# First loads in one queue in order of need, first gate matmuls by halves of K, parameters transposed once

## The chip, the cores and the metric

The kernel runs on one core of a Trainium2 chip. The metric is the device time in microseconds of that core. The TensorE clock granted by the throttle was 1.0. This record does not show PE's slow start: it reads 1.00 between 3 and 4 us in the kernel before, where matmuls of 512 columns still start 0.43 us apart. So PE's clock is read here from the spacing of its matmuls. A profile gives the same execution in detail: PE is the matmul engine, DVE the vector engine, ACT the scalar engine (ScalarE), POOL the Pool engine and SP the engine that issues most DMAs (SyncE). Profile times start about 1.8 us after the measured time does, so 180.6 us measured is a span of 178.8 us.

## The reference

One layer with two branches on the same normalized input, 2048 tokens of 512 channels:

```python
xn = _layernorm(x, axis=-1)
return x + _A_ref(xn, ...) + _B_ref(xn, w_gate, w_up, w_down)
# _B_ref: (silu(xn @ w_gate) * (xn @ w_up)) @ w_down, inner width 1376
# _A_ref: a diagonal complex state-space layer: two input projections, a scan over the
#         2048 steps, two output projections, a skip term
```

## The kernel before

The tokens are handled in four chunks of 512. A small static scheduler in the kernel file builds a graph of tasks. PE and SP run their tasks in the order in which they are added; the orders on ACT, DVE and POOL are chosen by the scheduler from estimated durations, then fixed. Each engine takes its list in that order, so a task that waits holds everything behind it.

The head, the part in question, works on chunk 0. Each x tile has 128 tokens. DVE computes its statistics, POOL the inverse standard deviation, DVE the normalized tile; PE transposes it into PSUM; ACT evacuates that to `xnT`. In four "quarters" (one per x tile) PE then multiplies six tiles of `wg` (`w_gate`) with the tile.

Some words used below: K is the dimension that a matmul sums over, here 512 channels in four pieces of 128. An evacuation copies a result of PE out of its PSUM bank, so that the kernel can use the bank again. Warm-up (or bridge) matmuls multiply constants and their results are thrown away; they fill PE's time while it waits for the first loads. "Landed" is when all of a load had arrived.

```python
dma("ld_x0", ...)                                   # SP queue: x0 x1 x2 wg0 x3 wu0 ...
dma("ld_x1", ...)
act_load("ld_wgA0", wg[:, 0:2, 0:FQ], ...)          # ACT queue, 256 KB: first half of K, 4 tiles
dma("ld_x2", ...)
act_load("ld_wgA1", wg[:, 2:4, 0:FQ], ...)          # ACT queue, 256 KB: second half of K
dma("ld_wg0", wg[:, :, FQ:FH0], ...)                # tiles 4 and 5
dma("ld_x3", ...)
# two of three small parameter loads follow on the ACT queue
...
# ffn_gate_quarters, shortened
for q in range(4):
    for ii, (i, bk) in enumerate(tiles):            # six tiles
        if q == 0 and ii == 2:
            params_t(tiles[-1][1])                  # three parameter transposes
        if q < 3 and ii == (4 if q == 0 else 2):
            xt_tile_fine(q + 1)                     # transposes of the next x tile
        # four matmuls of 128x128x128; they need both wg halves
```

Two parts far behind the head:

```python
# a DMA transpose waits for all DMAs before it; a DMA after it waits for the transpose
if xpose:
    after = after + tuple(dma_tasks)
elif xp_state[0] is not None:
    after = after + (xp_state[0],)
...
loads_stage_b1()        # two DMA transposes (B_re, B_im)
xt_chunk_dma(1)         # one DMA transpose (x of chunk 1)
loads_stage_b2()        # two DMA transposes (C_re, C_im), then ld_x8: x of chunk 2
...
def ln_apply_act(a0):   # chunks 2 and 3: normalization on ACT
    # DVE: nmr = -mean * rstd
    for a in range(a0, a0 + 4):
        # ACT: xn_sb[a] = x_sb[a] * rstd + nmr
```

Of the kernel before, what the change touches and what calls it, by code (L numbers as in the profile page):

```python
# [19 lines left out]
    warm=10,  # L20
# [218 lines left out]
def bass_parallel_sum__ssm_conv_s5__swiglu_ffn__prompt_kernel(  # L239
# [32 lines left out]
    with es:  # L272
# [46 lines left out]
        prow = sb("prow", [4, 3, 128], B16)  # L319
# [76 lines left out]
        def pload(name, slot, src, order=()):  # L396
            return dma(name, prow[:, slot, :], src.rearrange("(a p) -> a p", p=128), [("prow", slot)], 1024, eng="act", order=order)
        FQ = 4 * 128
        act_q = [pload("ld_ldt", 2, A_log_dt)]

        def act_load(*args):
            act_q.append(dma(*args, eng="act", order=(act_q[-1],)))
# [3 lines left out]
        act_load("ld_wgA0", wg[:, 0:2, 0:FQ], wg_v[:, 0:2, 0:FQ], [("wg", "a0")], 256 * FQ * 2)  # L406
        dma("ld_x2", x_sb[:, 2:3, :], x_v[:, 2:3, :], [("x", 2)], TILEB)
        act_load("ld_wgA1", wg[:, 2:4, 0:FQ], wg_v[:, 2:4, 0:FQ], [("wg", "a1")], 256 * FQ * 2)
        dma("ld_wg0", wg[:, :, FQ:FH0], wg_v[:, :, FQ:FH0], [("wg", 0)], 512 * (FH0 - FQ) * 2)
        dma("ld_x3", x_sb[:, 3:4, :], x_v[:, 3:4, :], [("x", 3)], TILEB)  # L410
        act_q.append(pload("ld_lim", 1, A_Lambda_im, (act_q[-1],)))
        act_q.append(pload("ld_lre", 0, A_Lambda_re, (act_q[-1],)))
# [41 lines left out]
        def params_t(slot):  # L454
            def tr(e):
                for k in range(3):
                    inst = e.transpose(out=ptr[:, slot, 4 * k:4 * k + 4], in_=prow[0:4, k, :], identity=ident[0:4, 0:4])  # L457
                return inst
            g.add("pe", tr, reads=[("prow", k) for k in range(3)] + [("ident",)], writes=BK(slot), name="parT", est=100, ninst=3)

        def params_ev(slot, order):
            return g.add("dve", lambda e: e.tensor_copy(out=praw[:].rearrange("p k a -> p (k a)"), in_=ptr[:, slot, 0:12]),
                         reads=BK(slot), writes=[("praw", k) for k in range(3)], name="parTev", est=80, order=order)
# [17 lines left out]
        def ln_apply(a, parts=1, order=()):  # L481
            w = D // parts
            for h in range(parts):
                cs = slice(h * w, (h + 1) * w)
                last = g.add("dve", lambda e, a=a, cs=cs: e.tensor_scalar(out=xn_sb[:, a % NXN, cs], in0=x_sb[:, a, cs], scalar1=mv[:, a, 0:1], scalar2=rstd[:, a:a + 1],
                                                                          op0=ALU.subtract, op1=ALU.mult),
                             reads=[("x", a), ("mv", a), ("rstd", a)], writes=([("xn", a % NXN)] if h == parts - 1 else []) + ([("xh", h)] if parts > 1 else []),
                             name="xn%d" % a, est=90 + 260 // parts, order=order)
            return last
# [10 lines left out]
        def ln_chunk0():  # L500
            bn_st(0)
            bn_ag(0)
            last = ln_ve(0, 1)
            ln_rstd(0, 1)
            last = ln_apply(0, parts=2, order=(bn_st(1, order=(last,)),))
            last = ln_ve(1, 1, order=(bn_ag(1, order=(last,)),))
            ln_rstd(1, 1)
            return bn_st(2, order=(last,))

        def ln_chunk0_rest(last, par_bank):  # L510
            last = ln_apply(1, order=(last,))
            for a in range(2, 4):
                last = ln_ve(a, 1, order=(bn_ag(a, order=(last,)),))
                hold[a] = ln_rstd(a, 1)
                if a == 2:
                    last = params_ev(par_bank, (last,))
                last = ln_apply(a, order=(bn_st(a + 1, order=(last,)),) if a < 3 else (last,))
# [15 lines left out]
        def xt_tile_fine(a, parts=1, wbank=None):  # L533
            n = KT // parts
            for h in range(parts):
                if h:
                    pe_warm(1, 256, wbank)
                slot = xt_pair[0] + (a + h) % 2

                def tr4(e, h=h, slot=slot):  # L540
                    for j in range(n):
                        kt = h * n + j
                        inst = e.transpose(out=ptr[:, slot, j * 128:(j + 1) * 128],  # L543
                                           in_=xn_sb[:, a % NXN, kt * 128:(kt + 1) * 128], identity=ident[:])
                    return inst
                g.add("pe", tr4, reads=([("xn", a % NXN)] if h == parts - 1 else []) + ([("xh", h)] if parts > 1 else []) + [("ident",)], writes=BK(slot), name="xT%d" % a, est=n * 64, ninst=n)

                def evac(e, h=h, slot=slot):
                    return e.activation(out=xnT[:, 0, a % 4, h * n:(h + 1) * n, :],  # L549
                                        in_=ptr[:, slot, 0:n * 128].rearrange("p (k t) -> p k t", k=n), func=AF.Identity)  # L550
                g.add("act", evac, reads=BK(slot), writes=([("xnT", 0, a % 4)] if h == parts - 1 else []) + ([("xnT0", h)] if parts > 1 else []), name="xTev%d" % a, est=190 + 310 // parts)
# [68 lines left out]
        def params_b():  # L620
            dve_ts("thT", "thn", float(TP), ALU.mult)
            dve_range("thn")
            dve_range("thT")
            for i, n in enumerate(["lre", "lim"]):
                o = S(n)
                small("dve", n, lambda e, o=o, i=i: e.tensor_copy(out=o, in_=praw[:, i, :]), [("praw", i)], R(n))
            dve_tt("lam_re", "r", "cos_thn", ALU.mult)
            dve_tt("lam_im", "r", "sin_thn", ALU.mult)
            dve_ts("lm1", "lam_re", -1.0, ALU.add)
            dve_tt("lre2", "lre", "lre", ALU.mult)  # L630
            dve_tt("lim2", "lim", "lim", ALU.mult)
            dve_tt("den", "lre2", "lim2", ALU.add)
            o, a_ = S("rden"), S("den")
            small("dve", "rden", lambda e, o=o, a_=a_: e.reciprocal(out=o, in_=a_), R("den"), R("rden"))
            dve_tt("n1", "lm1", "lre", ALU.mult)
            dve_tt("n2", "lam_im", "lim", ALU.mult)
            dve_tt("n3", "n1", "n2", ALU.add)
            dve_tt("g_re", "n3", "rden", ALU.mult)
            dve_tt("n4", "lam_im", "lre", ALU.mult)
            dve_tt("n5", "lm1", "lim", ALU.mult)  # L640
            dve_tt("n6", "n4", "n5", ALU.subtract)
            dve_tt("g_im", "n6", "rden", ALU.mult)
            dve_ts("s_2gre", "g_re", 2.0, ALU.mult)
            dve_ts("s_m2gim", "g_im", -2.0, ALU.mult)
            dve_ts("s_m2gre", "g_re", -2.0, ALU.mult)
# [51 lines left out]
        def wres(nm, i):  # L697
            if nm == "wg" and i < 4:
                return [("wg", "a0"), ("wg", "a1")]
            return [(nm, 0 if i < 6 else 1)]  # L700
# [34 lines left out]
        def ffn_gate_quarters(pairs, last):  # L735
# [3 lines left out]
            xt_tile_fine(0, parts=2, wbank=banks[pairs[-1]])  # L739
            pe_warm(3, 256, banks[pairs[-1]])  # L740
            tiles = [(2 * ip + k, banks[ip] + k) for ip in pairs for k in range(2)]
            for q in range(4):
                for ii, (i, bk) in enumerate(tiles):
                    if q == 0 and ii == 2:
                        params_t(tiles[-1][1])
                        ln_chunk0_rest(last, tiles[-1][1])
                    if q < 3 and ii == (4 if q == 0 else 2):
                        xt_tile_fine(q + 1)
                    for k0, k1 in (((0, 2), (2, 4)) if q == 0 and ii == 0 else ((0, 4),)):
                        def mm(e, bk=bk, i=i, q=q, k0=k0, k1=k1):  # L750
                            for kt in range(k0, k1):
                                inst = e.matmul(pbank[:, bk, q * 128:(q + 1) * 128], lhsT=wg[:, kt, i * 128:(i + 1) * 128], rhs=xnT[:, 0, q, kt, :],  # L752
                                                start=(kt == 0), stop=(kt == KT - 1))
                            return inst
                        xr = [("xnT", 0, q)] if q else [("xnT0", h) for h in range((k1 + 1) // 2)]
                        g.add("pe", mm, reads=wres("wg", i) + xr, writes=BK(bk), name="mm_gq%d_%d" % (i, q), est=(k1 - k0) * 56, ninst=k1 - k0)
# [165 lines left out]
        if _CFG["warm"]:  # L922
            pe_warm(_CFG["warm"])
        ffn_gate_quarters([0, 1, 2], ln_chunk0())
# [106 lines left out]
```

## Time and profile before

Before the prediction: 180.56 us, median of 3 runs (180.40 to 181.02).

| what | value | where it is read |
|---|---|---|
| span of the profiled run | 178.8 us | first line of the page |
| PE busy | 174.5 us, 98% | engine shares |
| first gate matmul | 6.35 us | chain of waits |
| first up matmul | 13.05 us | timeline of PE |
| wait for an evacuation before quarter 1 | 0.41 us | spacing of PE's matmuls |

Two lines of the page of the kernel before: its span, and busy time with the share of the span for each engine.

```profile
span 178.8 us, 2346 instructions
PE 174.5 (98%) x908; PEld 82.9 (46%) x908; DVE 160.6 (90%) x272; ACT 86.5 (48%) x107; POOL 13.0 (7%) x24
```

The chain of waits of the kernel before, followed back from its end. Columns: start in us, length in us, what the end was waiting for.

```profile
1.80 4.42 DMA wg<-in_B_w_gate_dram
...
6.35 0.61 PE pb L752 x8
6.96 0.16 PE pb L457 x3
...
7.92 0.61 ACT xnT L549
...
8.58 0.62 PE pb L752 x8
...
10.98 2.23 PE pb L752 x40
13.22 12.09 PE pb L713 x56
...
41.83 8.74 PE pb L713 x40
50.57 0.04 issue
50.60 8.81 PE pb L713 x40
```

L752 is the gate matmuls of the quarters, L457 the parameter transposes, L549 the evacuation of a transposed x tile, L713 the later gate and up matmuls. The second wg half arrives at 6.2 us and the gates start; after a wait for ACT at 7.92 us everything seems to be PE.

### The profile page before, as it was taken

The page shows a single profiled execution, that of the slowest core. Times are in us where ns is not written, and L with a number is a line of the kernel's source. Part 1 is how long each engine was busy: PE and PEld are TensorE (multiplying, and loading weights), DVE is VectorE, ACT ScalarE, POOL GpSimd, SP SyncE. Part 2 cuts the span into 40 slices and gives each one's busy share as a digit, 9 for nine tenths or more (in the row PEclk, how much of TensorE's full clock was granted, in tenths as well). Part 3 has the DMA queues.
Part 4 walks back from the last instruction along what each step waited for, and adds up shares of the span by engine and source line. Part 5 has one row for each costly group of instructions (what it writes and reads, how often), then busy time and mean ns, then how long its engine had stood idle before and what let it go on. Part 6 is the DMA issues. An engine that isn't in the chain of part 4 may idle for free.

```text
span 178.8 us, 2346 instructions
## 1 busy us (share of the span) xinstructions
PE 174.5 (98%) x908; PEld 82.9 (46%) x908; DVE 160.6 (90%) x272; ACT 86.5 (48%) x107; POOL 13.0 (7%) x24
## 2 busy tenths in 40 slices
PE   8799999999999999999999999999999999999994
PEld 2594444444444444444444444444444444444643
DVE  3888759998799999999999999999999999999733
ACT  3379899899696992060565651000965620000000
POOL 3362300001300000210000000000000000000000
DMA  5995646669360000002330000001100000001212
GB/s 159 353 355 110 129 81 72 148 170 354 113 117 4 0 0 0 0 0 92 85 64 0 0 0 4 0 0 59 59 0 4 0 0 0 0 0 33 69 48 88
DMA packets 23410, 12.37 MB, mean 69 GB/s; under 512 B 15112, under 2 KB 23400, under 8 KB 23400
## 3 DMA queue, kind: packets, MB, share of 16 engines
q1 hardware_dynamic: 22832, 11.70, 24.6%
q10 hardware_dynamic: 568, 0.53, 1.0%
q8 instruction: 7, 0.11, 0.3%
q14 instruction: 3, 0.02, 0.0%
HBM read 6.46 MB, written 2.10 MB: 48 GB/s over the span
## 4 chain that ended last, share of the span: by engine, by line
PE 95%; DMA 2%; ACTq 1%; ACT 0%; DVE 0%; issue 0%
PE pb L713 36%; PE pb L900 21%; PE pb L913 15%; PE pb L818 15%; PE pb L752 3%; DMA wg<-in_B_w_gate_dram 2%; PE pb L781 2%; PE pb L791 1%; ACTq L385 1%; PE pb L543 0%; ACT xnT L549 0%; DVE x_sb L918 0%; PE pb L457 0%
## 5 line engine op out<-in xcount | busy, mean ns | idle before, releaser
L858 DVE TENSOR_TENSOR_SCAN rot<-sm,car,rot 128x512 bf16<-128x512 f32 x32 | 39.1, 1268 | 0.1
L900 PE MATMUL pb<-wd,hT 128*128 128x512 bf16 (+3 forms) x187 | 38.7, 367 | 0.0
L713 PE MATMUL pb<-xnT,wu 128*128 128x512 bf16 x160 | 37.3, 379 | 0.0
L713 PE MATMUL pb<-xnT,wg 128*128 128x512 bf16 x136 | 32.0, 380 | 0.0
L913 PE MATMUL pb<-W,hss 128*128 128x512 bf16 (+1 forms) x136 | 28.3, 367 | 0.0
L818 PE MATMUL pb<-xnT,BT 128*128 128x512 bf16 x128 | 28.1, 379 | 0.0
L900 PEld LDWEIGHTS pb<-wd,hT 128*128 128x128 bf16 (+1 forms) x187 | 18.2, 97 | 20.1
L725 ACT ACTIVATE sg<-pb 128x1024 bf16<-128x1024 f32 x20 | 20.2, 1021 | 10.5 <-PE pb L713 10.2
L713 PEld LDWEIGHTS pb<-xnT,wu 128*128 128x128 bf16 x160 | 15.5, 98 | 18.9 <-ACT uf L771 0.5
L771 ACT ACTIVATE uf<-pb 128x1024 bf16<-128x1024 f32 x20 | 20.4, 1021 | 7.1 <-PE pb L713 5.7
L713 PEld LDWEIGHTS pb<-xnT,wg 128*128 128x128 bf16 x136 | 13.1, 98 | 16.4 <-issue 0.8
L913 PEld LDWEIGHTS pb<-W,hss 128*128 128x128 bf16 x136 | 13.3, 98 | 14.4
L818 PEld LDWEIGHTS pb<-xnT,BT 128*128 128x128 bf16 x128 | 12.5, 98 | 15.1
L825 ACT ACTIVATE u_sb<-pb 128x1024 bf16<-128x1024 f32 x16 | 16.3, 1025 | 3.9 <-PE pb L818 3.5
L918 DVE TENSOR_TENSOR x_sb<-pb,x_sb 128x512 bf16<-128x512 f32 (+1 forms) x17 | 10.9, 655 | 5.0 <-PE pb L913 5.0
L773 DVE TENSOR_TENSOR hT<-sg,uf 128x1024 bf16<-128x1024 bf16 x20 | 13.4, 677 | 2.1 <-ACT uf L771 2.1
L466 DVE BATCH_NORM_STATS2 st<-x_sb 128x6 f32<-128x512 bf16 x16 | 10.2, 681 | 5.0 <-DMA x_sb<-in_A_x_dram 5.0
L495 ACT ACTIVATE xn_sb<-x_sb,nmr,rstd 128x512 bf16<-128x512 bf16 x8 | 5.9, 802 | 10.5 <-DVE nmr L492 10.5
L800 ACT ACTIVATE sg<-pb 96x1024 bf16<-96x1024 f32 x2 | 2.0, 1019 | 17.4 <-PE pb L781 17.4
L849 DVE TENSOR_TENSOR rot<-rot,sin 128x2048 bf16<-128x2048 bf16 x8 | 9.8, 1219 | 0.0
L849 DVE TENSOR_TENSOR rot<-u_sb,sin 128x2048 bf16<-128x2048 bf16 x8 | 9.7, 1218 | 0.0
L849 DVE TENSOR_TENSOR rot<-u_sb,cosT 128x2048 bf16<-128x2048 bf16 x8 | 9.7, 1215 | 0.0
(71 smaller groups left out, 138.8 us busy)
## 6 DMA issues: line engine op xcount, KB each, us to landing
out_dram<-x_sb SPq DMA_DIRECT2D x15, 128.0 KB, 1.7
x_sb<-in_A_x_dram SPq DMA_DIRECT2D x3, 512.0 KB, 7.5
wd<-in_B_w_down_dram SPq DMA_DIRECT2D x1, 1280.0 KB, 7.0
wu<-in_B_w_up_dram SPq DMA_DIRECT2D x1, 768.0 KB, 6.1
wg<-in_B_w_gate_dram SPq DMA_DIRECT2D x1, 608.0 KB, 7.5
wu<-in_B_w_up_dram SPq DMA_DIRECT2D x1, 608.0 KB, 8.6
x_sb<-in_A_x_dram SPq DMA_DIRECT2D x4, 128.0 KB, 2.8
wg<-in_B_w_gate_dram ACTq DMA_DIRECT2D x2, 256.0 KB, 3.8
```

Of the source, the lines that this page charges most:

```text
L466: return g.add("dve", lambda e, a=a: e.bn_stats(out=st[:, a, :], in_=x_sb[:, a, :]), reads=[("x", a)], writes=[("st", a)], name="bnst%d" % ...
L713: inst = e.matmul(pbank[0:fs, bk, :].rearrange("p (j t) -> p j t", j=4), lhsT=w[:, kt, i * 128:i * 128 + fs], rhs=xnT[:, c % 2, :, kt, :], ...
L725: g.add("act", lambda e: e.activation(out=sg[rows, sl, 0:n, :].rearrange("p a t -> p (a t)"), in_=pair_f32(rows, bk, 512 * n), func=AF.Sil ...
L771: g.add("act", lambda e: e.activation(out=uf[rows, ul, 0:n, :].rearrange("p a t -> p (a t)"), in_=pair_f32(rows, bk, 512 * n), func=AF.Ide ...
L773: g.add("dve", lambda e: e.tensor_tensor(out=hT[rows, hb, i0:i0 + n, :], in0=sg[rows, sl, 0:n, :], in1=uf[rows, ul, 0:n, :], op=ALU.mult), ...
L818: inst = e.matmul(pbank[:, bk, :].rearrange("p (j t) -> p j t", j=4), lhsT=BT[:, ri, kt, pt * 128:(pt + 1) * 128], rhs=xnT[:, c % 2, :, kt ...
L825: g.add("act", lambda e: e.activation(out=u_sb[:, us].rearrange("p r t -> p (r t)"), in_=pair_f32(slice(0, 128), b0), func=AF.Identity), r ...
L849: tt = lambda out, a, b, op, r, w, nm: g.add("dve", lambda e: e.tensor_tensor(out=out, in0=a, in1=b, op=op), reads=r, writes=w, name="%s_% ...
L858: g.add("dve", lambda e, A0=A0, A1=A1, k=k, ri=ri, pt=pt: e.tensor_tensor_scan(out=A1[:, k, ri, :], data0=rr[:, pt:pt + 1].to_broadcast([1 ...
L900: inst = e.matmul(pbank[:, bk, 0:nc_], lhsT=hT[0:fs, hb, i, lt * 128:(lt + 1) * 128], rhs=wd[0:fs, i, c0:c0 + nc_], start=(i == 0), stop=F ...
L913: inst = e.matmul(pbank[:, bk, 0:nc_], lhsT=hss[:, hb, pt, ri, lt * 128:(lt + 1) * 128], rhs=W12[:, ri, pt, c0:c0 + nc_], start=False, sto ...
L918: g.add("dve", lambda e, bk=bk, a=a, c0=c0, nc_=nc_: e.tensor_tensor(out=x_sb[:, a, c0:c0 + nc_], in0=pbank[:, bk, 0:nc_], in1=x_sb[:, a, ...
```

## The change

Its intent: issue the first loads in one queue in the order in which they are needed, so that no later load competes with an earlier one; let the first gate matmuls start when half of the first x tile and half of wg are there; and take the parameter transposes out of the gate matmuls. The diff, cut to its core:

```diff
-            return dma(name, prow[:, slot, :], ..., eng="act", order=order)
+            return dma(name, prow[4 * slot:4 * slot + 4, :], ..., eng="act", order=order)
         act_q = [pload("ld_ldt", 2, A_log_dt)]
+        act_q.append(pload("ld_lim", 1, A_Lambda_im, (act_q[-1],)))
+        act_q.append(pload("ld_lre", 0, A_Lambda_re, (act_q[-1],)))
         dma("ld_x0", ...)
         dma("ld_x1", ...)
-        act_load("ld_wgA0", wg[:, 0:2, 0:FQ], ...)
+        dma("ld_wgA0", wg[:, 0:2, 0:FH0], ...)       # 384 KB, all six tiles
         dma("ld_x2", ...)
-        act_load("ld_wgA1", wg[:, 2:4, 0:FQ], ...)
-        dma("ld_wg0", wg[:, :, FQ:FH0], ...)
+        dma("ld_wgA1", wg[:, 2:4, 0:FH0], ...)
         dma("ld_x3", ...)
...
+            pe_warm(8, bk=wbank)
+            params_t(pbk)                # one transpose of 12 rows instead of three of 4
+            ln_chunk0(pbk)               # DVE: xn0 half, bn_aggr and eps of tile 1, xn0 half
+            pe_warm(2, bk=wbank)
+            xt_tile_fine(0, bridge=wbank)
+            pe_warm(2, 256, wbank)
             for q in range(4):
-                for ii, (i, bk) in enumerate(tiles):
-                    if q == 0 and ii == 2:
-                        params_t(tiles[-1][1])
-                    if q < 3 and ii == (4 if q == 0 else 2):
+                if q < 3:
+                    steps = [(i, bk, 2 * kh, 2 * kh + 2) for kh in range(2) for i, bk in tiles]
+                else:
+                    steps = [(i, bk, 0, 4) for i, bk in tiles]
+                for n, (i, bk, k0, k1) in enumerate(steps):
+                    if q < 3 and n == 9:
                         xt_tile_fine(q + 1)     # now two halves: 2 transposes and an evacuation each
```

## The prediction

> **What bounds the kernel now.** Engine shares on the page: PE busy 174.5 of 178.8 us (98%). The chain of waits is PE alone from 10.98 to 176.33 us; PE's timeline has no gap after the first up matmul (13.05 us). DVE is 90% busy, but its last hss tile is ready near 164.8 us and first read at 169.2 us. So the change can win only in the first 13 us, and the win should reach the end.
>
> **The head before** (timeline and chain). Warm-up to 4.7 us; the first x tile transposed at 5.15 and 5.41 us; its second ScalarE evacuation ends at 6.13 us; the first gate matmul starts at 6.35 us, because the second half of wg landed at 6.2 us. Then 108 matmuls and transposes at 56 ns (6.04 us), parameter transposes (0.15 us), one wait for an evacuation (8.17 to 8.58 us, 0.41 us): 13.05 us.
>
> **What changes.**
> - Loads in one queue. The Trainium skill, "DMA: Bandwidth & Descriptors", section "Issuing engines are not separate DMA queues", says that queues share the same 16 engines; this trace agrees (320 to 390 GB/s with one queue or two). By bytes I estimate the wg halves at 4.5 to 4.8 and 5.7 to 6.2 us, needed at 6.0 and 6.7 us. The DMA wait goes, worth only about 0.2 us. The small loads (two landed at 6.6 and 6.8 us behind wg) land near 3 us, so they don't hold PE.
> - Parameter transpose moved into idle time: 0.15 us less on PE later.
> - DVE does bn_aggr and the eps add of tile 1 (0.18 and 0.15 us) between the halves of tile 0: the second half comes near 5.63 instead of 5.35 us. With two bridge matmuls behind it I estimate the first gate matmul at 6.02 us: 0.33 us earlier.
> - Transposes by halves. Before, 16 or more matmuls covered an evacuation (0.60 us) in later quarters. Now only 6 matmuls (0.34 us) follow the next tile's transposes. A half's evacuation takes 0.38 us and starts 0.3 us after its transposes: I estimate waits of 0.19 us before quarters 1 and 2. Quarter 3 runs with full K and needs both halves at once: about 0.48 us. Sum 0.86 against 0.41 us: 0.45 us given back.
>
> **Sum.** -0.33 - 0.15 + 0.45 = about 0; first up matmul at 12.9 us (12.6 to 13.4). Matmuls, DVE work and bytes stay the same; the static scheduler may reorder DVE and ACT, which DVE's slack should hide.
>
> **Predicted time** 180.3 us, range 179.7 to 180.9; chances: faster by over 2% 0.01, within 2% 0.96, slower 0.03.
>
> **What would show each step.** PE's timeline: first gate matmul near 6.0 us without a DMA wait; idle gaps before quarters 1, 2 and 3, the last the longest, put down to ScalarE; first up matmul 12.6 to 13.2 us; no gap afterwards. DVE: the first tile's second half at 5.3 us. DMA: the second wg half before 6.5 us.
>
> **What would make it wrong.** A single queue that starts slower (second wg half after 6.7 us). PE left at its slow clock: warm-up matmuls were 0.43 us apart until 4.1 us, 0.22 us after (the skill, "TensorE: Matmul & The Clock Gate", "What's actually happening", tells of half rate until some 3.4 us of activity; this trace agrees). ScalarE doing a table step (0.72 us) before the last x evacuation: quarter 3 would slip 0.7 us. A DVE order that uses up the hss slack.

## The result and the profile after

The changed kernel took 181.37 us, median of 6 runs (180.83 to 181.85); the kernel before 180.70 us (180.40 to 181.07, 6 runs). The ratio is 1.0033, with a 95% interval of 1.0015 to 1.0051. Ratios here are the mean time of one kernel's fast runs over that of the other's in the same rounds, so they are not quite the ratio of the medians. By the 2% rule that is "the same", as forecast; but the median lies 0.47 us above the range of the prediction. Two later measurements of the unaltered changed kernel gave 0.9993 (0.997 to 1.0015) and 1.0037 (0.9998 to 1.0077). Over all 18 runs of the changed kernel the mean is 181.20 us, over the 28 of the kernel before that stood beside them 180.84 us: the change costs about 0.2%.

The same two lines of the page, of the changed kernel:

```profile
span 179.1 us, 2337 instructions
PE 174.8 (98%) x897; PEld 83.2 (46%) x905; DVE 160.2 (89%) x271; ACT 86.8 (48%) x111; POOL 12.7 (7%) x24
```

(Eight matmul records are missing from this trace, which has 897 matmuls for 905 weight loads. The change itself takes away three, two parameter transposes and a warm-up.) The shares say nothing. The timeline of PE in the head of the changed kernel does; columns: start, length, engine, line, what, count, and in brackets idle time and what ended it. L536 is the transposes of x, L444 the warm-up matmuls, L752 the gate matmuls of the quarters, L707 the first up matmuls.

```profile
5.28 0.42 PE L536 MATMUL pb<-ident,xn_sb 128*128 128x128 bf16 x2
5.49 0.42 PE L444 MATMUL pb<-const-bfloat16-1.0 128*128 128x256 bf16 x1
5.70 0.42 PE L536 MATMUL pb<-ident,xn_sb 128*128 128x128 bf16 x2
5.92 0.62 PE L444 MATMUL pb<-const-bfloat16-1.0 128*128 128x256 bf16 x2
6.34 1.29 PE L752 MATMUL pb<-xnT,wg 128*128 128x128 bf16 x18
...
11.01 0.39 PE L536 MATMUL pb<-ident,xn_sb 128*128 128x128 bf16 x4
11.23 0.50 PE L752 MATMUL pb<-xnT,wg 128*128 128x128 bf16 x6
12.23 1.51 PE L752 MATMUL pb<-xnT,wg 128*128 128x128 bf16 x24 [0.50 <-ACT xnT L542]
13.58 0.59 PE L707 MATMUL pb<-xnT,wu 128*128 128x512 bf16 x2
```

Three things can be read. The gates start at 6.34 us, no earlier than before: PE is still at its slow clock (two warm-up matmuls of 256 columns take 0.43 us from start to start of the next, 0.21 each; at the full clock it was 0.11 each), so the two that stand ahead of the gates take twice as long. Behind the transposes at 11.01 us stand only six matmuls, then PE idles for ACT. And the first up matmul starts at 13.58 us, 0.53 us later than before.

The chain of waits of the changed kernel:

```profile
3.22 4.54 DMA x_sb<-in_A_x_dram
...
7.78 0.69 DVE st L457
...
9.15 0.55 POOL rstd L469
9.70 1.00 POOL sm L602
...
10.91 0.72 ACT scrC L654
11.63 0.55 ACT xnT L542 x2
...
12.23 1.51 PE pb L752 x24
13.74 12.09 PE pb L707 x56
...
42.35 17.37 PE pb L707 x80
```

The chain no longer begins with wg but with x3, the fourth x tile, issued at 3.22 us and landed at 7.76 us. Its statistics on DVE, two steps on POOL and the first step of a sine table on ACT (L654) follow; that table step stands ahead of the last x evacuation in ACT's list and delays it. In the last line the row of L707 from 42.35 us runs through 80 matmuls: the break near 50 us is not there.

What the 16 DMA engines moved, in stretches of 1 us. Columns: stretch, its length, busy time of each engine (instructions), PE clock, mean busy share of the DMA engines, GB/s. First the kernel before:

```profile
3.00:4.00 1.00, 1.00 (x4) 0.36 (x3) 0.93 (x4) 0.89 (x1) 0.00 (x0) 1.00 1.02 335
6.00:7.00 1.00, 0.68 (x12) 0.58 (x11) 0.89 (x4) 0.13 (x1) 0.27 (x1) 1.00 1.07 348
```

Then the changed kernel:

```profile
3.00:4.00 1.00, 1.00 (x4) 0.21 (x2) 0.93 (x4) 0.49 (x2) 0.00 (x0) 1.00 0.83 171
6.00:7.00 1.00, 1.00 (x16) 0.83 (x13) 0.87 (x2) 0.50 (x2) 0.05 (x1) 1.00 1.03 289
```

In this pair of profiles the loads start slower with one queue: 171 instead of 335 GB/s between 3 and 4 us. The second profile of the kernel before had only 247 GB/s there.

### The profile page after: what moved, and what is told of

It is laid out like the page before. It is cut to its first block, busy times and chain, and to the rows that moved or that the text cites. A ratio compares the mean times of both kernels' runs of the same rounds, so it can differ in the third digit from the quotient of the medians.

```text
span 179.1 us, 2337 instructions
## 1 busy us (share of the span) xinstructions
PE 174.8 (98%) x897; PEld 83.2 (46%) x905; DVE 160.2 (89%) x271; ACT 86.8 (48%) x111; POOL 12.7 (7%) x24
## 4 chain that ended last, share of the span: by engine, by line
PE 92%; DMA 3%; SPq 1%; DVE 1%; POOL 1%; ACT 1%; issue 1%
PE pb L707 36%; PE pb L901 21%; PE pb L819 15%; PE pb L914 15%; DMA x_sb<-in_A_x_dram 3%; PE pb L782 2%; SPq L384 1%; PE pb L792 1%; PE pb L752 1%; POOL sm L602 1%; ACT scrC L654 0%; DVE st L457 0%; ACT xnT L542 0%; POOL rstd L469 0%; DVE x_sb L919 0%
## 5 line engine op out<-in xcount | busy, mean ns | idle before, releaser
L901 PE MATMUL pb<-wd,hT 128*128 128x512 bf16 (+3 forms) x183 | 38.0, 366 | 0.2
L707 PE MATMUL pb<-xnT,wu 128*128 128x512 bf16 x160 | 37.3, 379 | 0.0
L707 PE MATMUL pb<-xnT,wg 128*128 128x512 bf16 x136 | 32.0, 379 | 0.0
L707 PEld LDWEIGHTS pb<-xnT,wu 128*128 128x128 bf16 x160 | 15.6, 98 | 18.7 <-ACT uf L772 0.2
L707 PEld LDWEIGHTS pb<-xnT,wg 128*128 128x128 bf16 x136 | 13.1, 98 | 16.4 <-issue 0.8
L914 PEld LDWEIGHTS pb<-W,hss 128*128 128x128 bf16 x136 | 13.3, 98 | 14.4
L774 DVE TENSOR_TENSOR hT<-sg,uf 128x1024 bf16<-128x1024 bf16 x20 | 13.3, 677 | 2.5 <-ACT uf L772 2.4
L481 ACT ACTIVATE xn_sb<-x_sb,nmr,rstd 128x512 bf16<-128x512 bf16 x8 | 5.9, 802 | 9.4 <-DVE nmr L478 9.4
L850 DVE TENSOR_TENSOR rot<-rot,cosT 128x2048 bf16<-128x2048 bf16 x8 | 9.7, 1214 | 0.0
```

Of the source, the lines that this page charges most:

```text
L707: inst = e.matmul(pbank[0:fs, bk, :].rearrange("p (j t) -> p j t", j=4), lhsT=w[:, kt, i * 128:i * 128 + fs], rhs=xnT[:, c % 2, :, kt, :], ...
L774: g.add("dve", lambda e: e.tensor_tensor(out=hT[rows, hb, i0:i0 + n, :], in0=sg[rows, sl, 0:n, :], in1=uf[rows, ul, 0:n, :], op=ALU.mult), ...
L850: tt = lambda out, a, b, op, r, w, nm: g.add("dve", lambda e: e.tensor_tensor(out=out, in0=a, in1=b, op=op), reads=r, writes=w, name="%s_% ...
L901: inst = e.matmul(pbank[:, bk, 0:nc_], lhsT=hT[0:fs, hb, i, lt * 128:(lt + 1) * 128], rhs=wd[0:fs, i, c0:c0 + nc_], start=(i == 0), stop=F ...
L914: inst = e.matmul(pbank[:, bk, 0:nc_], lhsT=hss[:, hb, pt, ri, lt * 128:(lt + 1) * 128], rhs=W12[:, ri, pt, c0:c0 + nc_], start=False, sto ...
```

## Theories and experiments

- **A, loads.** The single queue moves less in the first microseconds; x2, the second wg half and x3 come late and hold PE, DVE and the parameter chain.
- **B, order on PE.** Only six matmuls stand behind each transpose, and quarter 3 needs both halves at once: about 0.86 us of waits whatever the loads do.
- **C, chance.** The moment at which PE's clock rises, and the loads, vary from run to run.
- **D, a second limit.** Something near 50 us takes back what the head wins.

Any edit moves the scheduler's estimates and with them the orders on DVE and ACT in the whole program. So in each experiment the order lists of ACT, DVE and POOL were pinned by task name to those of the kernel it starts from, and only the stated difference was made:

```python
for _e, _names in _PIN.items():
    _by = defaultdict(list)
    for _t in streams[_e]:
        _by[_t.name].append(_t)
    streams[_e] = [_by[_n].pop(0) for _n in _names.split()]
```

A summary first. "First gate", "first up" and "last" are starts of matmuls on PE in the one profiled run (us). "Waits" are PE's before quarters 1, 2 and 3, read as the distance between two matmuls less the usual 0.056 us; "near 50" is the same for the break near 50 us, less 0.216 us. All were computed from the packed traces; the last digit can differ by one from the timelines. Waits elsewhere in the head are not in this table. The median and the ratio to the kernel before of the same rounds come from 6 runs (4 where marked).

| run | first gate | waits | first up | near 50 | last | median | ratio (95%) |
|---|---|---|---|---|---|---|---|
| kernel before, first profile | 6.35 | 0.41 | 13.05 | 0.20 | 176.04 | 180.70 | |
| changed kernel, first profile | 6.34 | 0.19 0.19 0.67 | 13.58 | 0 | 176.36 | 181.37 | 1.0033 (1.0015 to 1.0051) |
| after_again | 6.35 | 0.19 0.19 0.47 | 13.29 | 0.23 | 176.30 | 180.74 | 0.9993 (0.997 to 1.0015) |
| after_third | 6.35 | 0.19 0.19 0.47 | 13.83 | 0.13 | 176.74 | 181.60 | 1.0037 (0.9998 to 1.0077) |
| before_again | 6.05 | 0.41 | 13.25 | 0.80 | 176.84 | 180.57 | 0.9986 (0.9953 to 1.0019) |
| before_one_queue | 6.72 | 0.41 | 13.44 | 0 | 176.22 | 181.13 | 1.0032 (0.9994 to 1.0069) |
| before_one_queue_narrow (4) | 7.35 | 0.41, and 0.44 before quarter 3 | 14.51 | 0 | 177.28 | 181.58 | 1.0056 (1.0038 to 1.0073) |
| before_one_queue_late_small (4) | 7.17 | 0.41 | 14.04 | 0 | 176.81 | 181.33 | 1.0043 (1.0028 to 1.0058) |
| after_two_queues | 6.45 | 0.19 0.19 0.47 | 14.86 | 0 | 177.64 | 182.17 | 1.0084 (1.0053 to 1.0115) |
| after_fast_loads | 6.20 | 0.19 0.19 0.47 | 13.11 | 0.17 | 176.07 | 180.91 | 1.0006 (0.9975 to 1.0037) |
| after_order | 6.09 | none for ACT | 12.90 | 0.21 | 175.90 | 180.58 | 0.999 (0.9956 to 1.0023) |
| after_best | 6.43 | none | 12.45 | 0.67 | 175.91 | 180.47 | 0.9992 (0.9953 to 1.0031) |
| before_free | 6.35 | 0.41 | 13.24 | 0 | 176.02 | 180.41 | 0.9975 (0.9943 to 1.0006) |
| after_free | 6.11 | 0.19 0.19 1.05 | 14.02 | 0 | 176.79 | 181.03 | 1.0002 (0.9969 to 1.0036) |
| best_free | 6.38 | none | 12.58 | 0 | 175.35 | 180.42 | 0.9972 (0.9939 to 1.0006) |
| order_free | 6.17 | none for ACT | 12.85 | 0 | 175.62 | 180.11 | 0.9959 (0.9925 to 0.9993) |
| best_columns | 6.03 | none for ACT | 12.52 | 0 | 175.30 | 180.29 | 0.9992 (0.9969 to 1.0016) |

The table can be checked against itself: last less first up is 162.78 us plus the wait near 50 us, in all 17 profiles, to within 0.02 us. So two of the three profiles of the changed kernel waited there too, 0.23 and 0.13 us.

### Noise: after_again, before_again, after_third

No edit.

> The changed kernel again, unaltered, for a second profile and for the size of the noise. In its first profile PE's warm-up matmuls stayed 0.43 us apart until 6.4 us (4.1 us in the kernel before), and x2, the second wg half and x3 landed at 6.1, 7.1 and 7.8 us, 0.9 to 1.2 us later than I had estimated by bytes. If the slow start of the loads belongs to the single queue, this profile shows again under 260 GB/s between 3 and 4 us and x3 after 7.3 us, and a ratio of 1.002 to 1.005. If it was the chance of one run, x3 lands near 6.6 us. If the moment at which PE's clock rises is chance, it falls somewhere else between 4.1 and 7.6 us; if the change sets it, it is 6.4 us again.

> The kernel before, unaltered, timed against itself: a null test. Ratio 1.000, and the width of its interval is the noise that every other comparison has to be read with (I expect plus or minus 0.002). Its profile gives a second moment for the rise of PE's clock. So far this was 3.7 to 4.3 us in three profiles and 6.2 to 6.7 us in three, of both kernels' families; if it is chance it may come early or late here. Where it is late, first gate matmul still at 6.3 to 6.5 us here, since that waits for the second wg half.

> The changed kernel a third time (the first two measurements said 1.0033 and 0.9993). If the change has an effect of its own of +0.3% the ratio is 1.002 to 1.005; if it is worth nothing within the noise, 0.998 to 1.002. Profile: waits before quarters 1, 2, 3 of 0.19, 0.19 and 0.47 us or more; first gate matmul at 6.1 us if PE's clock rises before 5 us, at 6.35 us if it rises after 6 us.

The null test gave 0.9986 with a half width of 0.0033: more noise than I had expected, and as wide as the effect in question. after_again met neither of its two forecasts for the loads: the 152 GB/s between 3 and 4 us spoke for the single queue, but x3 landed at 7.03 us (after 7.3 expected), and the ratio was 0.9993 (1.002 or more expected). Quarter 3 waited 0.47 us there; in after_third x3 landed at 7.87 us and PE waited 0.49 us for the second wg half in the middle of quarter 0. The first fast matmul came at 6.4, 6.4 and 6.5 us in the three profiles of the changed kernel, which looked like a property of the change; but after_free, with the same warm-up matmuls, had it at 5.4 us, after_order at 4.3 us, and before_free, with the warm-up of the kernel before, at 6.8 us. Over all 17 profiles it lies between 3.8 and 6.8 us (where PE stood idle just then, it can have risen up to 1 us before). I take it for chance (theory C). In the changed kernel a late rise moves the first gate matmul from 6.1 us (after_order, after_free) to 6.35 us, since slow warm-up matmuls stand in front of it. The kernel before has such matmuls there too, and waits for both wg halves besides; what ends later shows. In its first profile the clock was early and wg landed at 6.21 us: 6.35 us. In before_again wg landed at 6.00 us: 6.05 us. In before_free wg had landed at 5.75 us, but the clock was late, and PE was busy with slow warm-up matmuls (L481) until the gates (L783; asked for 4.6 to 6.7 us):

```profile
5.71 0.85 PE L481 MATMUL pb<-const-bfloat16-1.0 128*128 128x256 bf16 x3
6.35 0.56 PE L783 MATMUL pb<-xnT,wg 128*128 128x128 bf16 x4
```

So a late clock can cost both kernels some 0.3 us, and one profile of each says little about a difference of that size.

before_again also showed a cost that the change does remove: there the parameter transposes waited for a small load that landed at 6.97 us, and PE stood still for 0.58 us.

### The loads: after_two_queues, before_one_queue

```diff
 after_two_queues, against the changed kernel
-        dma("ld_wgA0", wg[:, 0:2, 0:FH0], ...)
+        act_load("ld_wgA0", wg[:, 0:2, 0:FH0], ...)      # and ld_wgA1: ACT queue, after the small loads
 before_one_queue, against the kernel before
-        act_load("ld_wgA0", wg[:, 0:2, 0:FQ], ...)
+        dma("ld_wgA0", wg[:, 0:2, 0:FH0], ...)           # and ld_wgA1: SP queue, loads as in the change
```

> The changed kernel with its two wg halves issued from ScalarE's queue again, after the three small loads; the order of instructions on ScalarE, DVE and Pool is pinned to that of the changed kernel. Theory A (the single queue starts slowly and its late x2, wg and x3 hold DVE, the parameter chain and so quarter 3): x3 lands before 7.2 us instead of 7.8, the small table step on ScalarE ends before the last x evacuation is due, first up matmul 0.3 to 0.7 us earlier than 13.58, total 0.3 to 0.6 us below the changed kernel. Theory B (the loss is the order on PE: too few matmuls behind each transpose, quarter 3 with full K): the waits before quarters 1, 2, 3 stay 0.19, 0.19 and at least 0.48 us, total within 0.2 us of the changed kernel.

> The kernel before with the load order of the changed kernel alone (both wg halves, 768 columns wide, in SyncE's queue), all other orders pinned to the kernel before. Here the first gate matmul needs both wg halves. Theory A: the second half lands at 7.0 us or later instead of 6.2, the first gate matmul starts 0.6 us or more after 6.35, total 0.4 to 0.9 us above the kernel before. If the single queue is not to blame: second half by 6.3 us, total within 0.2 us.

after_two_queues missed what theory A expected, by far: 182.17 us. PE's timeline shows one large wait in the middle of quarter 0:

```profile
8.61 0.51 PE L787 MATMUL pb<-xnT,wg 128*128 128x128 bf16 x6 [1.33 <-DMA wg<-in_B_w_gate_dram]
```

The second wg half landed at 8.56 us. ACT issued the two halves only at 2.03 and 2.48 us, behind three small loads, while SP, freed of them, issued the 768 KB of `wu` at 2.65 us, 1.1 us earlier than in the changed kernel. As I read it, the two queues then shared the engines and a load that nobody needed yet slowed the one that PE waited for: the second half was issued 0.27 us earlier than in the changed kernel and landed 1.48 us later. That speaks for the intent of the change, order of need. It is not shown by itself, since no run held back `wu` alone.

before_one_queue went as theory A expected, less strongly than it said: second wg half at 6.68 us (7.0 or later expected), first gate matmul at 6.72 us instead of 6.35 (6.95 or later expected), ratio 1.0032 with an interval that still takes in 1.

### What is slow about the one queue: before_one_queue_narrow, before_one_queue_late_small

```diff
 before_one_queue_narrow, against the kernel before
-        act_load("ld_wgA0", wg[:, 0:2, 0:FQ], ...)       # and ld_wgA1
+        dma("ld_wgA0", wg[:, 0:2, 0:FQ], ...)            # same size, SP queue
 before_one_queue_late_small, against before_one_queue
-        act_q.append(pload("ld_lim", ...)); act_q.append(pload("ld_lre", ...))    # ACT queue
+        pload("ld_lim", ...); pload("ld_lre", ...)       # SP queue, behind ld_x3
```

> The kernel before with its wg loads in SyncE's queue between the x tiles, but as narrow as before (two of 256 KB with rows of 1024 bytes, one of 256 KB with rows of 512 bytes). If one queue is itself the cause: 155 to 215 GB/s between 3 and 4 us, x3 at 7.2 us or later, second wg half after 6.3 us. If the wide rows are: over 230 GB/s between 3 and 4 us and x3 by 7.2 us. Ratio 0.999 to 1.004.

> before_one_queue with two of the three small loads moved from ScalarE's queue (where they ran at 1.8 to 3.7 us) to SyncE's, behind x3. If the small loads beside the single queue slow it down: over 230 GB/s between 3 and 4 us. If not: 155 to 215 GB/s as in the other profiles with one queue. The parameter transpose may now hold PE until 7.4 us, so the ratio (1.002 to 1.008) says nothing here.

With the old, narrow rows the second wg half landed at 7.21 us and x3 at 8.74 us, and PE waited longest of all for its first gate matmul:

```profile
7.35 0.61 PE L783 MATMUL pb<-xnT,wg 128*128 128x128 bf16 x8 [1.31 <-DMA wg<-in_B_w_gate_dram]
```

With the small loads out of the way the second half landed at 7.12 us and the rate between 3 and 4 us was 213 GB/s, as expected if they are not to blame. So nothing speaks for the wide rows or the small loads as the cause. All three kernels with one queue measured 0.3 to 0.6% slower, but their ratios are weaker evidence than the landings: the interval of before_one_queue takes in 1, the narrow variant has one load more ahead of x3, and its quarter 3 waited too (0.44 us), and in late_small the parameter transposes waited 0.24 us for the small loads, as its expectation warned. The rate between 3 and 4 us was not the clean mark I had taken it for: the narrow variant moved 252 GB/s there and then only 213 to 224 GB/s until 7 us. The landing of x3 is the better mark: 7.0 to 8.7 us, mean 7.8, in the nine profiles with one queue; 6.8 to 7.6 us, mean 7.1, in the seven that issue wg early from ACT. (after_two_queues, whose wg came late, is in neither.)

Issue time is the likeliest reason. The trace shows it directly: SP needs 0.40 to 0.48 us for each load, so with one queue the second wg half is issued at 2.75 us instead of 1.80 us and x3 at 3.22 us instead of 2.66 us. Landings follow by about as much. In the eight profiles that issue x3 near 3.2 us from one queue it landed at 7.66 us on average, in the six that issue it near 2.66 us at 7.04 us: 0.56 us in issue, 0.62 us in landing. The second wg half at equal size (384 KB) was issued near 2.75 and at 2.18 us and landed at 7.05 us (eight profiles) and 6.59 us (three) on average. No run delayed an issue on purpose, so this is read off and not tested.

Something else varies as well, which I can't explain: in the trace's packet records, the time above the usual for packets that took at least 60 ns too long sums to 8 to 10 us over the 16 engines before 7 us in two profiles of the kernel before and in that of before_free, and to 13 to 20 us in all others. As the two-queue variants of the changed kernel are among these, it does not tell one queue from two.

### Loads and order on PE, two by two: after_order, after_fast_loads, after_best

```diff
 after_order, against the changed kernel
-                    if q < 3 and n == 9:
+                    if q < 3 and n == 6:            # 12 matmuls behind the transposes, not 6
-                else:
-                    steps = [(i, bk, 0, 4) for i, bk in tiles]      # quarter 3 by halves too
   ACT order: table step tm0 behind the last x evacuation
 after_fast_loads, against the changed kernel
+        ACT queue: ld_ldt, ld_wgA0, ld_lim, ld_lre
+        SP queue:  ld_x0, ld_x1, ld_x2, ld_wgA1, ld_x3, ...
   params_t between the halves of the first x tile
 after_best: both, and
-            pe_warm(2, 256, wbank)
```

> The changed kernel, loads untouched, with the next x tile's transposes after step 6 of 12 instead of 9 (12 matmuls behind them instead of 6), quarter 3 by halves of K as well, and ScalarE's first table step after the last x evacuation; other orders pinned. Theory B: the waits before quarters 1 to 3 (0.19, 0.19, 0.67 us) fall to under 0.25 us in sum, but PE may wait for xn of tiles 1 and 2, which came late (up to 0.2 us each); first up matmul 0.5 to 0.9 us earlier than 13.58, total 0.4 to 0.9 us below the changed kernel. Theory A: PE then waits for DVE instead, because x2 and x3 are late, and the total is within 0.3 us of the changed kernel.

> The changed kernel, order on PE of the gate matmuls untouched, with the first wg half issued early from ScalarE's queue (beside x1 and x2 in SyncE's), the second wg half and x3 behind x2 in SyncE's queue; the parameters are transposed between the halves of the first x tile; orders pinned. By bytes, with two issuers from 1.4 us: second wg half near 6.0 us instead of 6.7 to 7.2, x3 near 6.3 us instead of 7.0 to 8.0. If late loads are what cost the changed kernel time: first up matmul 12.7 us or earlier, ratio 0.998 or less. If the order on PE is the limit: waits of 0.19, 0.19 and 0.47 us stay, first up matmul 12.95 to 13.3 us, ratio 0.999 to 1.002.

> The same loads as after_fast_loads, with the order on PE of after_order (transposes after step 6 of 12, quarter 3 by halves, ScalarE's table step after the last x evacuation), and without the two warm-up matmuls that stood between the first x tile and the first gate matmul. If order and loads limit together, as I think: waits before quarters 1 to 3 below 0.3 us in sum, first gate matmul near 5.95 us, first up matmul 12.1 to 12.4 us, that is 0.7 to 0.9 us before the kernel before, ratio 0.995 to 0.997. If something later in the program takes it back (DVE, ScalarE), PE shows new gaps after the first up matmul and the ratio is 0.998 or more.

The four kernels (changed, order alone, loads alone, both) have their first up matmul at 13.57 us (mean of 13.58, 13.29 and 13.83), 12.90, 13.11 and 12.45 us. In after_fast_loads PE's timeline shows the wait of quarter 3 untouched by the better loads:

```profile
10.96 0.50 PE L783 MATMUL pb<-xnT,wg 128*128 128x128 bf16 x6
11.77 1.51 PE L783 MATMUL pb<-xnT,wg 128*128 128x128 bf16 x24 [0.30 <-ACT xnT L574]
```

Theory B holds to the hundredth: 0.19, 0.19 and 0.47 us, whatever the loads did. In after_order those waits are gone. PE waits 0.23 us for the second wg half in quarter 0, and then for DVE, since tile 2 is normalized behind the statistics of the late x3:

```profile
9.10 0.40 PE L567 MATMUL pb<-ident,xn_sb 128*128 128x128 bf16 x4 [0.33 <-DVE xn_sb L504]
```

So A and B both show in the head: 0.67 us earlier by the order, 0.46 us by the loads, 1.12 us by both. These sizes are rough. Each is one profile against three that differ by 0.54 us among themselves, and after_order had an early clock, worth 0.26 us at its first gate matmul. In the measured times they do not stand apart: after_order (0.999) and the unaltered changed kernel in the same rounds (0.9993) are the same. The expectation for the loads was too good: x3 landed at 7.14 us, not 6.3 us. So was that for after_best: its first gate matmul came at 6.43 us, not 5.95 us, as x1 landed at 4.56 us (3.4 to 3.8 us in the others) and in DVE's list the statistics of tile 1 stand before the first half of tile 0.

But after_best won 0.60 us in the head (12.45 against 13.05 us) and its last matmul starts only 0.13 us earlier (175.91 against 176.04 us). PE's timeline near 50 us shows where the rest went:

```profile
48.08 1.89 PE L739 MATMUL pb<-xnT,wg 128*128 128x512 bf16 x8
50.48 1.68 PE L739 MATMUL pb<-xnT,wu 128*128 128x512 bf16 x7 [0.51 <-ACT uf L799]
```

### The second limit: before_free, after_free, best_free, order_free

Why does ACT come late there? The timeline of ACT in the kernel before:

```profile
44.21 1.02 ACT L725 ACTIVATE sg<-pb 128x1024 bf16<-128x1024 f32 x1
46.71 2.93 ACT L495 ACTIVATE xn_sb<-x_sb,nmr,rstd 128x512 bf16<-128x512 bf16 x4 [1.47 <-DVE nmr L492]
49.55 1.00 ACT L771 ACTIVATE uf<-pb 128x1024 bf16<-128x1024 f32 x1
```

ACT stands idle 1.47 us before four normalization steps of chunk 2, does them in 2.93 us, and only then empties the PSUM banks that PE needs. The steps wait for the statistics of chunk 2, and those for x8, which SP loads behind five DMA transposes that run one after the other. The page's list of DMA issues of the kernel before (what, engine, count, size in KB, us from issue to landing) has them:

```profile
xnT<-xn_sb SPq DMA_TRANSPOSE x3, 4.3
...
BT<-in_A_B_re_dram SPq DMA_TRANSPOSE x1, 4.3
BT<-in_A_B_im_dram SPq DMA_TRANSPOSE x1, 5.1
hss<-in_A_C_re_dram SPq DMA_TRANSPOSE x1, 5.0
hss<-in_A_C_im_dram SPq DMA_TRANSPOSE x1, 4.0
```

The chain starts when the last x tile of chunk 1 lands (14.21 us) and ends at PE's restart (50.60 us): five transposes until 37.31 us, x8 landed at 40.95 us, the last normalization done at 49.64 us. DVE took up x8 at once (it had stood idle 1.19 us for it) and the statistics went over POOL, so nothing in this chain waits for PE. In the four experiments the four steps move behind later evacuations, where ACT has time:

```diff
 order on ACT
-silu1_0 xn8 xn9 xn10 xn11 uev1_0 silu1_1 uev1_1 silu1_2 uev1_2
+silu1_0 uev1_0 silu1_1 xn8 uev1_1 xn9 silu1_2 xn10 uev1_2 xn11
```

before_free, after_free and best_free are the kernel before, the changed kernel and after_best with that; order_free is after_order with that and without the two warm-up matmuls.

> A second limit showed up in the profiles: near 50.5 us PE waits for a PSUM bank (0.2 us in the profile of the kernel before, 0.8 us in its second one, 0.67 us in after_best, 0 to 0.17 us with the changed kernel), because ScalarE stands in order before four layer-norm steps of chunk 2 that wait for x8, which SyncE loads only after five DMA transposes in a row. Here the kernel before has those four steps moved one by one behind later ScalarE evacuations; nothing else is changed. Theory of the second limit: no gap near 50 us, last PE work 162.8 us after the first up matmul (163.0 to 163.6 before), ratio 0.996 to 0.999. Rival (that gap is only where PE's lead is noticed and something else waits next): a new gap later, ratio 0.999 to 1.002.

> The same move of four ScalarE steps in the changed kernel. Its head ends later (first up matmul 13.3 to 13.8 us against 13.05 to 13.25), so the second limit costs it nothing or little: no more than 0.2 us better than the changed kernel, ratio to the kernel before 0.999 to 1.003; against before_free it should be 0.3 to 0.6 us slower, which is the true cost of the change in the head. If the second limit had nothing to do with the result, after_free and before_free stand to each other as the changed kernel and the kernel before.

> after_best with the same move of four ScalarE steps. after_best had its first up matmul at 12.45 us, 0.6 us before the kernel before, and gave 0.67 us back near 50 us. Theory of the second limit: no gap near 50 us, last PE work starts 162.8 us after the first up matmul (near 175.2 us instead of 175.9), ratio 0.993 to 0.996. If the gain is given back a second time, PE shows a new gap and the ratio is 0.997 or more.

> after_order (loads in one queue as in the changed kernel) without the two warm-up matmuls before the first gate matmul and with the same move of four ScalarE steps. Tells whether the single queue or the early ScalarE issue is better under the better order on PE. First gate matmul near 5.95 us (6.1 if PE's clock rises late), waits for the second wg half and for xn of tile 2 of 0 to 0.7 us depending on when wg and x3 land (6.7 to 7.2 and 7.0 to 8.0 us so far), first up matmul 12.2 to 12.9 us, ratio 0.994 to 0.998; within 0.002 of best_free if the queues don't matter.

(The first expectation gives the changed kernel 0 to 0.17 us of this wait; after_again had 0.23 us.) The break is gone in all four. PE in best_free:

```profile
48.20 1.89 PE L739 MATMUL pb<-xnT,wg 128*128 128x512 bf16 x8
49.93 1.89 PE L739 MATMUL pb<-xnT,wu 128*128 128x512 bf16 x8
```

and from the first up matmul to the last matmul of the program the four take 162.78, 162.77, 162.77 and 162.77 us (last less first up, from the table), so in these profiles nothing else takes anything back. With the break the kernel before took 162.99 and 163.59 us, after_best 163.46 us, after_order 163.00 us. Theory D holds for the traces: what the head wins reaches the last matmul once this wait is out of the way.

The measured times do not show it yet. best_free ended 0.67 us before before_free in the profiled runs, but over six runs each their medians are 180.42 and 180.41 us. By its ratio (0.9972, not 0.993 to 0.996) best_free even falls where its expectation put a gain given back again, though no new gap is in its trace. Its profile shows one thing that I overlooked: PE stood still in the head for a small parameter load, the cost that the change had removed and that the loads of after_fast_loads brought back by issuing wg ahead of the small loads.

```profile
6.17 0.16 PE L480 MATMUL pb<-ident,prow 12*128 12x12 bf16 x1 [0.61 <-DMA prow<-in_A_Lambda_re_dram]
```

after_free against before_free, run on the same chip, is 1.003 (mean of six runs each, 180.93 over 180.39 us, 0.54 us): the cost of the change in the head, at the size that theory D expected (0.3 to 0.6 us), without the wait near 50 us, which in the kernel before hides a part of it. Its profile came out worse than expected (first up matmul at 14.02 us, not 13.3 to 13.8): x3 landed at 8.19 us and the table step made quarter 3 wait 1.05 us.

order_free is the only version whose interval lies wholly below 1 (0.9959), 180.11 us against 180.81 us of the kernel before in its rounds. best_free (0.9972) and before_free (0.9975) are not clearly apart from it. One such interval among fifteen runs is weak evidence for a gain of 0.4%; what is firm is that the wait near 50 us is gone from the trace. Its single queue did not put it behind best_free, so the choice of queue is not settled for that order on PE.

### best_columns

```diff
 against best_free
-    ld_wgA0 and ld_wgA1: 768 columns each
+    ld_wgA0 (ACT queue) and ld_wgA1 (SP queue): 512 columns each; ld_wg0 with tiles 4 and 5 behind
+    quarter 0: tiles 0 to 3 by halves, transposes of tile 1, tiles 4 and 5
```

> best_free with narrower first loads: the first wg half for four tiles alone (256 KB) on ScalarE's queue, the second (256 KB) and the columns of tiles 4 and 5 behind x2 in SyncE's; in quarter 0 the four tiles run both halves of K first, tiles 4 and 5 after the transposes of tile 1. First gate matmul 5.95 us (6.2 if PE's clock is late), no wait for wg, first up matmul 12.1 to 12.5 us, last PE work 162.8 us later, ratio 0.993 to 0.997. If the narrower loads are no better, wg holds PE after quarter 0's first eight matmuls and the ratio is that of best_free, 0.997.

The gates started at 6.03 us and the first up matmul at 12.52 us, as expected, but PE waited 0.21 us for the second wg half, and the ratio was 0.9992: two of six runs took 180.9 us. Narrower loads are no better. The profiled run was among the good ones, which one profile cannot tell.

## Why the prediction was wrong where it was

- **"Same", within 2%.** Right.
- **180.3 us, range 179.7 to 180.9.** Wrong: 181.37 us. The range of 1.2 us was too narrow for six runs of a kernel whose head varies with the loads and the clock (medians of the unaltered changed kernel: 181.37, 180.74 and 181.60 us), and its centre was too low. A part of that is a slip: -0.33 - 0.15 + 0.45 is -0.03 us, which gives a first up matmul at 13.02 us and a time of 180.5 us, not 12.9 and 180.3. The rest are the terms below. They explain the profiled runs (180.83, 180.78 and 181.21 us). Why the other five runs of the first measurement took 181.1 to 181.85 us stays open, as none of them was profiled.
- **"By bytes I estimate the wg halves at 4.5 to 4.8 and 5.7 to 6.2 us."** This is the step that failed: the loads of a single queue were forecast too early. They landed at 5.77 and 7.08 us (5.24 and 6.67, 5.56 and 7.53 us in the other two), and x3 at 7.76, 7.03 and 7.87 us. I had counted bytes over the rate of a queue that is already running and left out that SP issues the second half only at 2.75 us. In the changed kernel "320 to 390 GB/s with one queue or two" is true between 4 and 6 us (337 to 392 GB/s in its three profiles), not between 3 and 4 us (152 to 186) nor between 6 and 7 us (192 to 345). "The DMA wait goes" was therefore wrong: waits of 0.08, 0 and 0.49 us inside quarter 0, and through the late x3 a table step on ACT that lengthened quarter 3's wait to 0.67 us, which the prediction had listed as a risk. before_one_queue has this step alone: second half at 6.68 us, first gate matmul 0.37 us later, ratio 1.0032 (0.9994 to 1.0069).
- **"First gate matmul at 6.02 us."** Right with an early clock (6.09 us in after_order, 6.11 us in after_free), 6.35 us with a late one, as in all three profiles of the changed kernel. The prediction named the clock as a risk and gave it no weight, though only 5 of 17 profiles had their first fast matmul before 5 us.
- **"Waits of 0.19 us before quarters 1 and 2, quarter 3 about 0.48 us."** Right: 0.19, 0.19, 0.47 us, in every profile with that order in which nothing else stood in front, and gone when 12 matmuls stood behind the transposes.
- **"0.15 us less on PE later" for the parameters.** Right in kind; in before_again the old place cost 0.58 us more.
- **First up matmul at 12.9 us.** It came at 13.58, 13.29 and 13.83 us. The mean is 13.57 us, 0.55 us after the 13.02 us of the prediction's own sum: 0.33 us were lost before the first gate matmul, mostly to the late clock, and 0.27, 0 and 0.49 us to the late loads (in quarter 0 and before quarter 3).
- **"PE's timeline has no gap after the first up matmul", "the win should reach the end".** Wrong, and in the prediction's own profile: 0.20 us near 50.4 us, 0.80 us in the second profile. I had looked at merged rows, which close over a wait of this size, and had checked DVE's slack at the end of the program but not ACT's in the middle. Here the error hid a loss rather than a gain: it is why the head lost 0.42 us on average in the profiles (13.57 against 13.15 us, the mean of 13.05 and 13.25), while the last matmul started at 176.47 us on average against 176.44 us: the changed kernel waited 0.12 us near 50 us on average, the kernel before 0.50 us.

What stays open: why most runs of the first measurement were slower than its profiled one, why packets take longer in most variants than in the kernel before, and what sets the moment at which PE's clock rises. That it is chance is an inference from 17 profiles; no run set it on purpose.

## What to carry to other kernels

A row of PE work without visible idle time can still hide a wait; compare the start-to-start distance of matmuls with the usual one all along the program before saying that a gain in the head reaches the end, and look for an engine that stands in order before work whose data come over a chain of serial DMAs. When work is cut into halves so that it starts earlier, count what is left behind each transfer: the time of an evacuation has to be covered by the matmuls after the transposes, or the start is paid back at every seam. And estimate the first microseconds of loads from landings seen with the same number of issuing queues, not from bytes over the full rate.

## What the Trainium skill lacked or had wrong

- "DMA: Bandwidth & Descriptors", section "Issuing engines are not separate DMA queues": it says that issuing from several engines only saves the issue time, "which is usually small relative to the DMA itself". At the start of this kernel it is not small: SP took 0.40 to 0.48 us per load, longer than 128 KB take at the 348 GB/s seen between 6 and 7 us in the kernel before (0.38 us), and x3, issued 0.56 us later with one queue than with two, landed 0.6 us later on average.
- "TensorE: Matmul & The Clock Gate", section "What's actually happening": it gives the moment of the clock's rise as varying by 500 ns to either side. In these 17 profiles, all with PE busy from 0.83 us, the first fast matmul lay between 3.8 and 6.8 us. (Further on the same section does say that the number of slow matmuls changes from run to run.)
- The same page, section "Part 4: PE-mode transpose", says that the full clock "doesn't engage" for transposes. Here they start 0.056 us apart at the full clock, like the matmuls beside them, and 0.107 us apart at the slow one. They stand among matmuls here; whether transposes alone would raise the clock no run shows.
- "DMA: Bandwidth & Descriptors", section "Latency and other measured facts", gives 261 GB/s for DMA transposes with a non-contiguous middle dimension, from one kernel, and more for contiguous ones. Run one after the other with a wait between, as here, 512 KB took 4.0 to 6.0 us from issue to landing, that is 87 to 131 GB/s; the page has no figure for that case, and it set the second limit of this kernel.
